# Sliding-window attention and sentence-level experts on one core: the first sentence alone to its gate, values behind their q/k, deeper prefetch, merged bank pairs, another slot order

## The chip, the cores and the metric

One core of one Trainium2 chip. The metric is the device time of an execution in microseconds (us); the span of a profile, from the first to the last instruction, is about 1.6 us shorter than the time of the same run. Engines: PE is the tensor engine (PEld its weight loads), DVE the vector engine, ACT the scalar engine, POOL GpSimd, SP the engine that here only issues transfers. With one core, a run is called slow when it takes over 1.5% longer than the fastest of the same kernel, so the label says how long it took, not why. Chips differ by a few tenths of a per cent (here, medians of the kernel before from 250.87 to 252.35 us); every kernel is therefore compared with runs of the kernel before on its own chip.

## The reference

```python
B, H, S, D = 8, 8, 576, 64          # q, k, v: float32
# 1. attention: causal, window of 64
scores = q @ k.T / 8 ;  keep 0 <= i - j < 64 ;  x = softmax(scores) @ v
# 2. one expert per sentence
x = x.transpose(0, 2, 1, 3).reshape(8, 576, 512)
logits = x.mean(axis=1) @ w_gate    # [8 sentences, 8 experts]
e = argmax(logits) ;  gate = softmax(logits)[e]
out = gate * (relu(x @ w1[e]) @ w2[e])          # w1: 512 x 1024, w2: 1024 x 512
```

In this draw the sentences choose the experts 5, 4, 2, 7, 1, 5, 7, 2. w1 is loaded eight times. w2 is kept on the core and loaded only at an expert's first use, so five times.

## The kernel before

A sentence is five units of attention: four pairs of heads (query rows 0 to 511), and one unit for the last 64 rows of all heads. For each pair: load q/k (POOL queue, cast to fp16 on the way) and values (SP queue), transpose q and k on PE, copy them out of PSUM, scores (`st_s`), exponential (ACT), mask (DVE), product with the values (`st_a`), division by the sum (DVE), transpose of the result (`st_x`). After five units the gate can be computed and the weights of the expert fetched. Expert work comes in chunks (`h_chunk`, 16 a sentence; `o_chunk`, 5 a sentence) that the program weaves between the pieces of attention, slot by slot.

```python
    qkp = tile_pool(name="qkp", bufs=6);  vp = tile_pool(name="vp", bufs=4)
    op_ = tile_pool(name="op", bufs=4)                     # output tiles
    ps_s = tile_pool(name="ps_s", bufs=1, space=PSUM)      # scores: 2 banks
    ps = tile_pool(name="ps", bufs=6, space=PSUM)          # everything else: 1 bank each
...
    def tr(n, part):                                       # half of a pair's q/k transposes
        tp = ps.tile([128, m, 2, 64], FP16, tag="b", name="tp")
        ...                                                # PE transposes into tp
        nc.vector.tensor_copy(out=qo, in_=tp[:, :, 0, :].rearrange("d t p -> d p t"))
        nc.scalar.copy(out=ko, in_=tp[:, :, 1, :].rearrange("d t p -> d p t"))
...
    def st_a(u, half):                                     # called twice a unit
        av = ps.tile([128, 512], FP32, tag="b", name="av")
        ...                                                # products; then reciprocal and multiply
...
    def o_chunk(i):                                        # i = 0..4
        ...                                                # 8 matmuls into po
        ob = op_.tile([128, Dm], FP32, tag="ob", name="ob")
        nc.vector.tensor_scalar(out=ob[0:n], in0=po[0:n], scalar1=gws[b][0:n, 0:1], ...)
        nc.sync.dma_start(out=out[b, 128 * i:128 * i + n, :], in_=ob[0:n])
...
        for s in range(NSLOT + 4):                         # START = 11: experts lag 11 slots
            st_a(s - 1, 0); st_a(s - 1, 1)
            fill(0.1)                                      # fill(p): expert chunks up to share p
            mask_it = st_s(s)
            fill(0.3)
            tr(n, 0);  mask_it()
            fill(0.5)
            st_x(s - 2)
            fill(0.75)
            tr(n, 1);  cast_v(n);  load_qk(n + 5);  load_v(n + 3)
            fill(1.0)
            if s >= 7 and (s - 7) % NU == 0: gate((s - 7) // NU)
            if s >= 8 and (s - 8) % NU == 0: gate2((s - 8) // NU)
```

The softmax here doesn't subtract the row's maximum and nothing guards it: scores larger than these inputs give would overflow.

## Time and profile before

| | kernel before |
|---|---|
| time, median of the first 6 runs | 251.97 us (249.93 to 252.39) |
| profiled span | 251.0 us |
| PE / DVE / ACT busy | 222.1 / 166.5 / 124.3 us |
| first expert matmul | 51.7 us |
| one sentence in the middle | 26.10 us |

The first view is the page of the kernel before: busy time of each engine, then PE in 40 slices of the span (tenths busy), then the clock granted to PE in the same slices.

```profile
PE 222.1 (89%) x2800; PEld 139.3 (56%) x2800; DVE 166.5 (66%) x525; ACT 124.3 (50%) x289; POOL 104.9 (42%) x191
...
PE   0476897779999999999999999999999998994992
...
PEclk9999999999999999999999999999999999999999
```

PE has gaps in the first nine slices and in the last seven, and none between. The windows of busy time of the kernel before (columns: stretch and length, then each engine's busy us and its number of instructions, granted clock, DMA share, GB/s) show one sentence of the middle:

```profile
106.34:132.44 26.10, 26.10 (x352) 15.92 (x352) 20.13 (x63) 15.00 (x37) 13.15 (x23) 1.00 1.11 219
```

PE is busy for all of it. The chain of waits of the kernel before (start, length, what) shows what bounds the ends:

```profile
7.65 12.99 DMA v_125<-in_v_dram
...
42.32 8.82 DMA w1t<-in_moe_w_dram
...
51.69 1.12 PE ph L327 x4
...
219.17 10.29 DMA w1t<-in_moe_w_dram
...
229.82 8.00 PE ph L327 x64
237.82 8.77 PE po L310 x40
```

The head waits for values, later for the first w1, and experts (`ph` is the first product, `po` the second) start at 51.7. The tail waits for the last w1.

The timeline of the kernel before (start, length, engine, line, operation, count, and in brackets the idle time before it with what ended it), one half of a pair's transposes:

```profile
108.30 0.41 PE L156 MATMUL tp<-ident,qk 128*64 128x128 f16 x8
...
108.75 0.44 DVE L161 COPY qT_151<-tp 128x256 f16<-128x256 f16 x1 [0.71 <-PE tp L156]
...
109.29 0.45 ACT L162 COPY kT_149<-tp 128x256 f16<-128x256 f16 x1 [0.30 <-DVE qT_151 L161]
```

ACT's copy of k starts 0.10 us after DVE's copy of q has ended, although it needs nothing from it. Both read the same PSUM tile.

### The profile page before, as it was taken

What the parts mean: (1) busy time and instruction counts of PE and PEld (TensorE: products, weight loads), DVE (VectorE), ACT (ScalarE), POOL (GpSimd) and SP (SyncE); (2) the same over time, 40 slices, a digit from 0 to 9 for tenths busy, and PEclk for the clock granted to TensorE, in tenths of its full rate; (3) what the DMA queues carried; (4) which work ended last, traced back from release to release, by engine and by line L of the source; (5) the groups of instructions that cost most, each with busy time, mean ns of one, the idle gap of its engine ahead of it and who ended that gap; (6) DMA issues with size and microseconds to landing.
All of it is one profiled execution on the core that took longest, in us unless ns stands there. A gap on an engine that the chain in (4) does not pass through costs nothing.

```text
span 251.0 us, 7513 instructions
## 1 busy us (share of the span) xinstructions
PE 222.1 (89%) x2800; PEld 139.3 (56%) x2800; DVE 166.5 (66%) x525; ACT 124.3 (50%) x289; POOL 104.9 (42%) x191
## 2 busy tenths in 40 slices
PE   0476897779999999999999999999999998994992
PEld 0364575546656665566556655665567546643741
DVE  3476898817687778776878787878686763441232
ACT  2265675636545764476537743764377425401500
POOL 7976996962195049514762468024500100000000
PEclk9999999999999999999999999999999999999999
DMA  6999999999399999999999999994930293087023
GB/s 123 209 206 185 200 178 190 185 204 207 67 153 217 199 306 147 222 200 298 164 216 199 293 170 206 199 296 81 216 115 4 31 207 123 1 146 209 3 86 102
DMA packets 59907, 42.45 MB, mean 169 GB/s; under 512 B 40416, under 2 KB 48608, under 8 KB 59872
## 3 DMA queue, kind: packets, MB, share of 16 engines
q0 software_dynamic: 16080, 23.07, 54.9%
q1 hardware_dynamic: 43792, 18.90, 30.0%
q8 instruction: 23, 0.38, 0.6%
q14 instruction: 12, 0.10, 0.1%
HBM read 61.88 MB, written 9.44 MB: 284 GB/s over the span
## 4 chain that ended last, share of the span: by engine, by line
PE 68%; DMA 16%; DVE 8%; SPq 3%; issue 2%; ACT 1%; POOLq 0%; DVEq 0%; ACTq 0%
PE ph L327 28%; PE po L310 21%; DMA w1t<-in_moe_w_dram 8%; PE tp L156 7%; DMA v_125<-in_v_dram 5%; PE sp L176 4%; PE av L211 3%; DMA out_dram<-ob 3%; PE xps L237 3%; SPq L77 2%; DVE x L195 2%; DVE pt L186 1%; PE av L220 1%; DVE ob L346 1%; PE gl L252 1%
## 5 line engine op out<-in xcount | busy, mean ns | idle before, releaser
L327 PE MATMUL ph<-xT,w1t 128*128 128x288 f16 x512 | 77.4, 292 | 6.4 <-DMA w1t<-in_moe_w_dram 5.4
L310 PE MATMUL po<-WT,hT 128*128 (+1 forms) x320 | 75.0, 380 | 0.0
L327 PEld LDWEIGHTS <-w1t 128*128 128x128 f16 x512 | 45.1, 99 | 20.8 <-DMA w1t<-in_moe_w_dram 6.1
L183 ACT ACTIVATE pt<-sp 128x1024 f16<-128x1024 f32 (+1 forms) x40 | 37.4, 935 | 24.1 <-PE sp L176 23.9
L332 ACT ACTIVATE hT<-ph 128x288 f16<-128x288 f32 x96 | 37.6, 413 | 22.6 <-PE ph L327 21.0
L310 PEld LDWEIGHTS <-hT 128*128 128x128 f16 (+1 forms) x320 | 29.9, 100 | 31.4 <-issue 0.8
L346 DVE TENSOR_SCALAR ob<-po,gw 128x512 f32<-128x512 f32 (+1 forms) x40 | 29.9, 748 | 23.6 <-PE po L310 20.9
L156 PE MATMUL tp<-ident,qk 128*64 128x128 f16 x576 | 33.1, 256 | 10.2 <-DMA qk<-in_k_dram 10.2
L195 DVE TENSOR_TENSOR x<-av,rl 128x256 f16<-128x256 f32 (+1 forms) x80 | 33.8, 423 | 2.7
L156 PEld LDWEIGHTS <-qk 128*64 128x64 f16 x576 | 22.1, 128 | 20.4 <-issue 17.8
L282 POOL DMA_DIRECT2D w1t<-in_moe_w_dram x8 | 6.0, 754 | 64.6 <-DVE x L195 42.1
L186 DVE TENSOR_TENSOR pt<-pt,mask 128x1024 f16<-128x1024 f16 (+1 forms) x40 | 27.0, 675 | 0.7 <-ACT pt L183 0.6
L239 ACT ACTIVATE xT<-xps 128x512 f16<-128x512 f16 x32 | 19.2, 601 | 14.7 <-PE xps L237 14.7
L334 DVE TENSOR_SCALAR hT<-ph 128x288 f16<-128x288 f32 x32 | 14.5, 452 | 17.2 <-PE ph L327 17.1
L66 POOL DMA_DIRECT2D qk<-in_q_dram x32 | 19.6, 613 | 13.8 <-PE av L211 8.1
L66 POOL DMA_DIRECT2D qk<-in_k_dram x32 | 19.5, 609 | 0.0
L211 PEld LDWEIGHTS <-pt 128*64 128x64 f16 x512 | 12.5, 122 | 9.9 <-DVE pt L186 8.1
L237 PE MATMUL xps<-ident,x 128*128 128x128 f16 (+1 forms) x160 | 16.7, 234 | 0.0
L237 PEld LDWEIGHTS <-x 128*128 128x128 f16 (+1 forms) x160 | 11.1, 105 | 8.9 <-issue 5.5
L194 DVE RECIPROCAL rl<-av 128x4 f32<-128x4 f32 (+1 forms) x80 | 13.6, 170 | 1.1 <-PE av L220 1.0
L162 ACT COPY kT_146<-tp 128x256 f16<-128x256 f16 (+1 forms) x12 | 5.5, 459 | 9.6 <-DVE qT_148 L161 9.4
L162 ACT COPY kT_149<-tp 128x256 f16<-128x256 f16 (+1 forms) x12 | 5.4, 452 | 8.6 <-DVE qT_151 L161 8.4
(234 smaller groups left out, 233.6 us busy)
## 6 DMA issues: line engine op xcount, KB each, us to landing
w1t<-in_moe_w_dram POOLq DMA_DIRECT2D x8, 1024.0 KB, 9.4
WT<-in_moe_w_dram POOLq DMA_DIRECT2D x8, 1024.0 KB, 15.0
out_dram<-ob SPq DMA_DIRECT2D x32, 256.0 KB, 7.1
qk<-in_q_dram POOLq DMA_DIRECT2D x32, 144.0 KB, 7.0
qk<-in_k_dram POOLq DMA_DIRECT2D x32, 144.0 KB, 8.1
out_dram<-ob SPq DMA_DIRECT2D x8, 128.0 KB, 5.5
v_100<-in_v_dram SPq DMA_DIRECT2D x2, 128.0 KB, 3.1
v_111<-in_v_dram SPq DMA_DIRECT2D x2, 128.0 KB, 7.5
```

What stands on the lines that cost most here:

```text
L66: nc.gpsimd.dma_start(out=t[64 * i:64 * i + 64].rearrange("p h t d -> p h (t d)"), in_=src[b, 2 * hp:2 * hp + 2, :, :].rearrange("h (p t) ...
L156: nc.tensor.transpose(out=tp[64 * hh:64 * hh + 64, t].rearrange("p a b -> p (a b)"), in_=qks[n][:, hh, lo + t, :], identity=ident)
L183: nc.scalar.activation(out=pv, in_=sp[:, :, 0:64 * m], func=AF.Exp, scale=scale)
L186: nc.vector.tensor_tensor(out=pv, in0=pv, in1=mk.unsqueeze(1).broadcast_to([128, 2, 64 * m]), op=ALU.mult)
L195: nc.vector.tensor_tensor(out=x.rearrange("p (g d) -> p g d", d=D), in0=avv[:, :, 0:D], in1=rl[0:n].broadcast_to([n, 4, D]), op=ALU.mult)
L211: nc.tensor.matmul(out=av[64 * jj:64 * jj + 64, o:o + D + 1], lhsT=pt[:, hh, 2 * i + jj, :], rhs=vx[:, 1 - jj, i, hh, :], start=True, stop ...
L237: nc.tensor.transpose(out=tp[:, g], in_=x[0:n, g, :], identity=ident[0:n, 0:n])
L239: nc.scalar.activation(out=xTs[b][:, c, 0:512], in_=tp.rearrange("p g t -> p (g t)"), func=AF.Copy, accum_out=pps[b][:, c:c + 1])
L310: m = nc.tensor.matmul(**kw)
L327: nc.tensor.matmul(out=ph[:, 0:SC], lhsT=w1v[:, kb, ft // 2, ft % 2, :], rhs=xTs[b][:, kb, ts(sc, SC)], start=(kb == 0), stop=(kb == NHP - 1))
L332: nc.scalar.activation(out=dst, in_=ph[:, 0:SC], func=AF.Relu)
L346: nc.vector.tensor_scalar(out=ob[0:n], in0=po[0:n], scalar1=gws[b][0:n, 0:1], scalar2=None, op0=ALU.mult)
```

## The change

Its intent: bring the first gate forward, so that PE gets expert work earlier; keep inputs ahead; and use fewer, larger instructions. The parts: (a) the five units of sentence 0 run alone, then its gate, and q/k go ahead of values in the first loads; (b) experts start at slot 8 for sentence 0 and lag 10 slots after that, gates follow the last unit at once, with the index going straight to w1's load; (c) deeper prefetch; (d) the merge: scores and products share two pairs of banks, one reciprocal and one multiply a unit, and each half of a pair's transposes is copied out, q and k together, by one engine; (e) another order inside a slot.

```diff
-    qkp = ... bufs=6    vp = ... bufs=4
+    qkp = ... bufs=10   vp = ... bufs=6
-    ps_s = ... bufs=1   ps = ... bufs=6
+    ps2 = ... bufs=2    ps = ... bufs=4
@@ load_v
+            if n < NHP:
+                tc.add_manual_dep(d.ins, qkd[n], SYNC, reason="order of the first loads")
@@ tr
-        nc.vector.tensor_copy(out=qo, in_=tp[:, :, 0, :].rearrange("d t p -> d p t"))
-        nc.scalar.copy(out=ko, in_=tp[:, :, 1, :].rearrange("d t p -> d p t"))
+        if part == 0:
+            nc.vector.tensor_copy(out=o, in_=i)          # q and k of this half
+        else:
+            nc.scalar.copy(out=o, in_=i)
@@ st_a: one call a unit
-        av = ps.tile([128, 512], FP32, tag="b", name="av")
+        av = ps2.tile([128, 2, 512], FP32, tag="s", name="av")
@@ the program (cut)
+        for u in range(1, NU + 2):                       # sentence 0 alone
+            tr(u, 0); mask_it(); tr(u, 1); mask_it = st_s(u); st_a(u - 1); cast_v(u)
+            ensure(min(u + 3, 7), min(u + 2, 6))         # q/k and values loaded so far ahead
+            st_x(u - 2)
+        gate(0)
+        for n in (NHP, NHP + 1): ensure(n + 4, n + 2); tr(n, 0); tr(n, 1); cast_v(n)
+        gate2(0); gate3(0)
+        for s in range(NU, NSLOT + 3):
+            rate = 2.4 if s < 15 else 3.3 if s < NSLOT - 6 else 2.4 if s < NSLOT else 1.2
+            st_a(s - 1); mask_it = st_s(s)
+            fill(0.4 * rate)
+            tr(n, 0); mask_it(); tr(n, 1); cast_v(n); ensure(n + 6, n + 4)
+            fill(0.3 * rate)
+            st_x(s - 2)
+            fill(0.3 * rate)
+            (gate and gate2 if s - 2 was a sentence's last unit, gate3 a slot later)
```

(Conditions at the ends, and the parts of the gate that only move, are cut.)

More of the change, by code (lines that the diff above doesn't have):

```diff
@@ L42 @@
     const = ctx.enter_context(tc.tile_pool(name="const", bufs=1))
-    qkp = ctx.enter_context(tc.tile_pool(name="qkp", bufs=6))
-    vp = ctx.enter_context(tc.tile_pool(name="vp", bufs=4))
+    qkp = ctx.enter_context(tc.tile_pool(name="qkp", bufs=10))
+    vp = ctx.enter_context(tc.tile_pool(name="vp", bufs=6))
     ptp = ctx.enter_context(tc.tile_pool(name="ptp", bufs=2))
@@ L51 @@
     gp = ctx.enter_context(tc.tile_pool(name="gp", bufs=2))
-    ps_s = ctx.enter_context(tc.tile_pool(name="ps_s", bufs=1, space=bass.MemoryType.PSUM))
-    ps = ctx.enter_context(tc.tile_pool(name="ps", bufs=6, space=bass.MemoryType.PSUM))
+    ps2 = ctx.enter_context(tc.tile_pool(name="ps2", bufs=2, space=bass.MemoryType.PSUM))
+    ps = ctx.enter_context(tc.tile_pool(name="ps", bufs=4, space=bass.MemoryType.PSUM))
     qks, v32s, v8s, xTs = {}, {}, {}, {}
     pts, xs, wts, gws, pps, eis, w1s = {}, {}, {}, {}, {}, {}, {}
+    qkd = {}
     NP = B * NHP
@@ L65, in load_qk @@
         for (i, src) in ((0, q), (1, k)):
-            nc.gpsimd.dma_start(
+            d = nc.gpsimd.dma_start(
                 out=t[64 * i:64 * i + 64].rearrange("p h t d -> p h (t d)"),
                 in_=src[b, 2 * hp:2 * hp + 2, :, :].rearrange("h (p t) d -> p h (t d)", t=TK))
+            qkd[n] = d.ins.name
     def load_v(n):
@@ L76, in load_v @@
         for hh in range(2):
-            nc.sync.dma_start(
+            d = nc.sync.dma_start(
                 out=t[:, :, hh, :],
                 in_=v[b, 2 * hp + hh, 0:512, :].rearrange("(i p) d -> p i d", p=128))
-        if hp == 0:
+            if n < NHP:
+                tc.add_manual_dep(d.ins, qkd[n], SYNC, reason="order of the first loads")
+        if hp == 3:
             t8 = vp.tile([128, H, D], FP32, tag="v8", name="v8", bufs=2)
@@ L92 @@
     load_qk(0)
-    load_v(0)
     nc.gpsimd.affine_select(out=ident, in_=ident, compare_op=ALU.not_equal, fill=1.0,
@@ L96 @@
     load_qk(1)
-    load_v(1)
+    load_qk(2)
     nc.gpsimd.affine_select(out=mask[0:64, 1:8], in_=mask[0:64, 1:8], compare_op=ALU.is_gt, fill=0.0,
@@ L101 @@
                             base=0, pattern=[[0, 8], [1, 64]], channel_multiplier=-1)
-    load_qk(2)
-    load_v(2)
     load_qk(3)
-    load_v(3)
-    load_qk(4)
+    for n in range(NHP):
+        load_v(n)
     wg = const.tile([128, NHP, E], FP32)
-    nc.sync.dma_start(out=wg, in_=moe_w_gate.rearrange("(kb p) e -> p kb e", p=128))
     iota = const.tile([1, E], FP32)
@@ L117 @@
     NT = 6
-    kTs, qTs = [], []
+    qkTs = []
     for m in range(NT):
-        t = const.tile([128, 64 + S], FP16, name=f"kT{m}")
-        nc.vector.memset(t[:, 0:64], 0.0)
-        kTs.append(t)
-        qTs.append(const.tile([128, S], FP16, name=f"qT{m}"))
+        t = const.tile([128, 2, 64 + S], FP16, name=f"qkT{m}")
+        nc.vector.memset(t[:, 1, 0:64], 0.0)
+        qkTs.append(t)
     NV = 4
@@ L158, in tr @@
                     in_=qks[n][:, hh, lo + t, :], identity=ident)
-        qo = qTs[n % NT].rearrange("d (p t) -> d p t", t=TK)[:, :, lo:hi]
-        ko = kTs[n % NT][:, 64:].rearrange("d (p t) -> d p t", t=TK)[:, :, lo:hi]
-        nc.vector.tensor_copy(out=qo, in_=tp[:, :, 0, :].rearrange("d t p -> d p t"))
-        nc.scalar.copy(out=ko, in_=tp[:, :, 1, :].rearrange("d t p -> d p t"))
+        o = qkTs[n % NT][:, :, 64:].rearrange("d a (p t) -> d a p t", t=TK)[:, :, :, lo:hi]
+        i = tp.rearrange("d t a p -> d a p t")
+        if part == 0:
+            nc.vector.tensor_copy(out=o, in_=i)
+        else:
+            nc.scalar.copy(out=o, in_=i)
     def st_s(u):
         b, c = divmod(u, NU)
-        sp = ps_s.tile([128, 2, 512], FP32, tag="s", name="sp")
+        sp = ps2.tile([128, 2, 512], FP32, tag="s", name="sp")
         pt = ptp.tile([128, 2, 8, 64], FP16, tag="pt", name="pt")
@@ L176, in st_s @@
                 nc.tensor.matmul(
-                    out=sp[:, hh, 64 * o:64 * o + 64], lhsT=kTs[n % NT][r, 64 * j:64 * j + 128],
-                    rhs=qTs[n % NT][r, 64 * j:64 * j + 64],
+                    out=sp[:, hh, 64 * o:64 * o + 64], lhsT=qkTs[n % NT][r, 1, 64 * j:64 * j + 128],
+                    rhs=qkTs[n % NT][r, 0, 64 + 64 * j:128 + 64 * j],
                     start=True, stop=True, tile_position=(64 * hh, 0), skip_group_check=True)
@@ L189, in st_s @@
         return apply_mask
-    def norm(u, av, n, x):
-        avv = av[0:n, 0:4 * (D + 1)].rearrange("p (g e) -> p g e", e=D + 1)
-        rl = gp.tile([128, 4, 1], FP32, tag="rl", name="rl")
-        nc.vector.reciprocal(out=rl[0:n], in_=avv[:, :, D:D + 1])
-        nc.vector.tensor_tensor(out=x.rearrange("p (g d) -> p g d", d=D), in0=avv[:, :, 0:D],
-                                in1=rl[0:n].broadcast_to([n, 4, D]), op=ALU.mult)
-    def st_a(u, half):
-        b, c = divmod(u, NU)
-        pt = pts[u]
-        if half == 0:
-            xs[u] = xp.tile([128, 4, 128], FP16, tag="x", name="x")
-        x = xs[u].rearrange("p i e -> p (i e)")[:, 256 * half:256 * half + 256]
-        av = ps.tile([128, 512], FP32, tag="b", name="av")
-        if c < NHP:
-            vx = vxs[(NHP * b + c) % NV]
-            for i in (2 * half, 2 * half + 1):
-                for hh in range(2):
-                    o = ((i % 2) * 2 + hh) * (D + 1)
-                    for jj in range(2):
-                        nc.tensor.matmul(
-                            out=av[64 * jj:64 * jj + 64, o:o + D + 1],
-                            lhsT=pt[:, hh, 2 * i + jj, :], rhs=vx[:, 1 - jj, i, hh, :],
-                            start=True, stop=True, tile_position=(0, 64 * jj),
-                            skip_group_check=True)
-            norm(u, av, 128, x)
-        else:
-            for g in range(4):
-                hp, hh = 2 * half + g // 2, g % 2
-                nc.tensor.matmul(
-                    out=av[0:64, g * (D + 1):(g + 1) * (D + 1)], lhsT=pt[:, hh, hp, :],
-                    rhs=vxts[b % 2][:, 2 * hp + hh, :], start=True, stop=True,
-                    skip_group_check=True)
-            norm(u, av, 64, x[0:64])
-        if half == 1:
-            pts.pop(u)
@@ new lines, in st_a @@
+    def st_a(u):
+        b, c = divmod(u, NU)
+        pt = pts.pop(u)
+        x = xp.tile([128, 4, 128], FP16, tag="x", name="x")
+        xs[u] = x
+        av = ps2.tile([128, 2, 512], FP32, tag="s", name="av")
+        n = 128 if c < NHP else 64
+        for g in range(8):
+            o = av[:, g // 4, (g % 4) * (D + 1):(g % 4 + 1) * (D + 1)]
+            i, hh = g // 2, g % 2
+            if c < NHP:
+                for jj in range(2):
+                    nc.tensor.matmul(
+                        out=o[64 * jj:64 * jj + 64], lhsT=pt[:, hh, 2 * i + jj, :],
+                        rhs=vxs[(NHP * b + c) % NV][:, 1 - jj, i, hh, :], start=True, stop=True,
+                        tile_position=(0, 64 * jj), skip_group_check=True)
+            else:
+                nc.tensor.matmul(out=o[0:64], lhsT=pt[:, hh, i, :], rhs=vxts[b % 2][:, g, :],
+                                 start=True, stop=True, skip_group_check=True)
+        avv = av[0:n, :, 0:4 * (D + 1)].rearrange("p a (g e) -> p a g e", e=D + 1)
+        rl = gp.tile([128, 2, 4, 1], FP32, tag="rl", name="rl")
+        nc.vector.reciprocal(out=rl[0:n], in_=avv[:, :, :, D:D + 1])
+        nc.vector.tensor_tensor(
+            out=x[0:n].rearrange("p i (h d) -> p (i h) d", d=D).rearrange(
+                "p (a g) d -> p a g d", a=2),
+            in0=avv[:, :, :, 0:D], in1=rl[0:n].broadcast_to([n, 2, 4, D]), op=ALU.mult)
@@ L256, in gate @@
         gm = gp.tile([1, 8], FP32, tag="gm", name="gm")
-        gi = gp.tile([1, 8], U32, tag="gi", name="gi")
+        gi = gp.tile([1, 8], U32, tag="gi", name="gi", bufs=4)
         nc.vector.max(out=gm, in_=gs)
         nc.vector.max_index(out=gi, in_max=gm, in_values=gs)
-        gf = gp.tile([1, 1], FP32, tag="gf", name="gf")
-        nc.vector.tensor_copy(out=gf, in_=gi[:, 0:1])
-        oh = gp.tile([1, E], FP32, tag="oh", name="oh")
-        nc.vector.tensor_scalar(out=oh, in0=iota, scalar1=gf, scalar2=None, op0=ALU.is_equal)
-        st2 = gp.tile([1, E], FP32, tag="st2", name="st2")
-        nc.vector.tensor_tensor(out=st2, in0=oh, in1=seen, op=ALU.mult)
-        nc.vector.tensor_tensor(out=seen, in0=seen, in1=oh, op=ALU.max)
-        ei = gp.tile([1, 2], U32, tag="ei", name="ei", bufs=4)
-        nc.vector.reduce_sum(out=gf, in_=st2, axis=AX.X)
-        nc.vector.tensor_copy(out=ei[:, 0:1], in_=gi[:, 0:1])
-        nc.vector.tensor_copy(out=ei[:, 1:2], in_=gf)
-        eis[b] = ei
         ereg = nc.gpsimd.alloc_register(f"er{b}")
-        nc.gpsimd.load(ereg, ei[0:1, 0:1])
-        hreg = nc.gpsimd.alloc_register(f"hr{b}")
-        nc.gpsimd.load(hreg, ei[0:1, 1:2])
+        nc.gpsimd.load(ereg, gi[0:1, 0:1])
         e = nc.gpsimd.snap(ereg, donate=True, min_val=0, max_val=E - 1)
-        have = nc.gpsimd.snap(hreg, donate=True, min_val=0, max_val=1)
         w1e = moe_w1.rearrange("e (kb p) f -> e p kb f", p=128)
-        w2e = moe_w2.rearrange("e (g p r) d -> e p g (r d)", p=128, r=2)
         w1t = wp.tile([128, NHP, F], FP16, tag="w1t", name="w1t")
@@ L282, in gate, with gate2 @@
         nc.gpsimd.dma_start(out=w1t, in_=w1e[ds(e, 1)].squeeze(0))
-        W2 = WT[:, ds(e, 1), :].squeeze(1).rearrange("p (g x) -> p g x", g=4)
-        mine = [nc.gpsimd.dma_start(out=W2, in_=w2e[ds(e, 1)].squeeze(0), cond=have < 1)]
-        for d in mine:
-            for other in tmms + loads:
-                tc.declare_no_dep(d.ins, other, reason="an expert is loaded before its first use")
-        loads.extend(d.ins.name for d in mine)
-        wts[b] = [d.ins.name for d in mine]
+        eis[b] = (gi, gs, gm, e)
+    def gate2(b):
+        gi, gs, gm, e = eis[b]
         nm = gp.tile([1, 1], FP32, tag="nm", name="nm")
@@ L297, in gate, with gate3 @@
         gws[b] = gr
-    def gate2(b):
+        gf = gp.tile([1, 1], FP32, tag="gf", name="gf")
+        nc.vector.tensor_copy(out=gf, in_=gi[:, 0:1])
+        oh = gp.tile([1, E], FP32, tag="oh", name="oh")
+        nc.vector.tensor_scalar(out=oh, in0=iota, scalar1=gf, scalar2=None, op0=ALU.is_equal)
+        st2 = gp.tile([1, E], FP32, tag="st2", name="st2")
+        nc.vector.tensor_tensor(out=st2, in0=oh, in1=seen, op=ALU.mult)
+        nc.vector.tensor_tensor(out=seen, in0=seen, in1=oh, op=ALU.max)
+        ei = gp.tile([1, 1], U32, tag="ei", name="ei")
+        nc.vector.reduce_sum(out=gf, in_=st2, axis=AX.X)
+        nc.vector.tensor_copy(out=ei, in_=gf)
+        hreg = nc.gpsimd.alloc_register(f"hr{b}")
+        nc.gpsimd.load(hreg, ei[0:1, 0:1])
+        have = nc.gpsimd.snap(hreg, donate=True, min_val=0, max_val=1)
+        w2e = moe_w2.rearrange("e (g p r) d -> e p g (r d)", p=128, r=2)
+        W2 = WT[:, ds(e, 1), :].squeeze(1).rearrange("p (g x) -> p g x", g=4)
+        mine = [nc.gpsimd.dma_start(out=W2, in_=w2e[ds(e, 1)].squeeze(0), cond=have < 1)]
+        for d in mine:
+            for other in tmms + loads:
+                tc.declare_no_dep(d.ins, other, reason="an expert is loaded before its first use")
+        loads.extend(d.ins.name for d in mine)
+        wts[b] = [d.ins.name for d in mine]
+    def gate3(b):
         glp = ps.tile([128, 1], FP32, tag="b", name="glp")
@@ L320, in h_chunk @@
                 pe = nc.tensor.alloc_register(f"pe{b}")
-                nc.tensor.load(pe, eis[b][0:1, 0:1])
+                nc.tensor.load(pe, eis[b][0][0:1, 0:1])
                 st["e"] = nc.tensor.snap(pe, donate=True, min_val=0, max_val=E - 1)
@@ L356, with ensure, start, fill @@
     NSLOT = B * NU
-    START = 11
-    RATE = 16.5 / NU
     chunks = []
+    spent = target = 0.0
+    qk_next, v_next = 4, 4
+    def ensure(nq, nv):
+        nonlocal qk_next, v_next
+        while qk_next <= min(nq, NP - 1):
+            load_qk(qk_next)
+            qk_next += 1
+        while v_next <= min(nv, NP - 1):
+            load_v(v_next)
+            v_next += 1
+    def start(b):
+        return 8 if b == 0 else NU * b + 10
+    def fill(amount):
+        nonlocal spent, target
+        target += amount
+        while chunks and spent < target:
+            cost, f = chunks.pop(0)
+            f()
+            spent += cost
+        if not chunks:
+            target = spent
     with tc.manual_schedule():
@@ L363 @@
         cast_v(0)
-        load_qk(5)
-        tr(1, 0)
-        tr(1, 1)
-        cast_v(1)
-        load_qk(6)
-        load_v(4)
-        spent = 0.0
-        for s in range(NSLOT + 4):
-            b, c = divmod(s, NU)
-            if s >= START and (s - START) % NU == 0 and (s - START) // NU < B:
-                chunks += list(moe_chunks((s - START) // NU))
-            def fill(part):
-                nonlocal spent
-                while chunks and spent < (s - START + part) * RATE:
-                    cost, f = chunks.pop(0)
-                    f()
-                    spent += cost
-            if 0 <= s - 1 < NSLOT:
-                st_a(s - 1, 0)
-                st_a(s - 1, 1)
-            fill(0.1)
+        nc.sync.dma_start(out=wg, in_=moe_w_gate.rearrange("(kb p) e -> p kb e", p=128))
+        mask_it = st_s(0)
+        for u in range(1, NU + 2):
+            if u < NHP:
+                tr(u, 0)
+                mask_it()
+                tr(u, 1)
+            elif u <= NU:
+                mask_it()
+            if u < NU:
+                mask_it = st_s(u)
+            if u <= NU:
+                st_a(u - 1)
+            if u < NHP:
+                cast_v(u)
+            ensure(min(u + 3, 7), min(u + 2, 6))
+            if u >= 2:
+                st_x(u - 2)
+        gate(0)
+        for n in (NHP, NHP + 1):
+            ensure(n + 4, n + 2)
+            tr(n, 0)
+            tr(n, 1)
+            cast_v(n)
+        gate2(0)
+        gate3(0)
+        for s in range(NU, NSLOT + 3):
+            b, c = divmod(s, NU)
+            for g in range(B):
+                if s == start(g):
+                    chunks += list(moe_chunks(g))
+            rate = 2.4 if s < 15 else 3.3 if s < NSLOT - 6 else 2.4 if s < NSLOT else 1.2
+            n = NHP * b + c + 2 if c < NHP else NP
+            if NU <= s - 1 < NSLOT:
+                st_a(s - 1)
             mask_it = st_s(s) if s < NSLOT else None
-            fill(0.3)
-            n = NHP * b + c + 2 if c < NHP else NP
+            fill(0.4 * rate)
             tr(n, 0)
@@ L392 @@
                 mask_it()
-            fill(0.5)
-            if 0 <= s - 2 < NSLOT:
-                st_x(s - 2)
-            fill(0.75)
             tr(n, 1)
@@ L399 @@
             if n < NP:
-                load_qk(n + 5)
-                load_v(n + 3)
-            fill(1.0)
-            if s >= 7 and (s - 7) % NU == 0:
-                gate((s - 7) // NU)
-            if s >= 8 and (s - 8) % NU == 0:
-                gate2((s - 8) // NU)
+                ensure(n + 6, n + 4)
+            fill(0.3 * rate)
+            if NU <= s - 2 < NSLOT:
+                st_x(s - 2)
+            fill(0.3 * rate)
+            if s > NU + 2 and (s - 2) % NU == 4:
+                gate((s - 2) // NU)
+                gate2((s - 2) // NU)
+            if s > NU + 3 and (s - 3) % NU == 4:
+                gate3((s - 3) // NU)
         for bb in range(B):
-            if START + NU * bb >= NSLOT + 4:
+            if start(bb) >= NSLOT + 3:
                 chunks += list(moe_chunks(bb))
```

## The prediction

> **What bounds the kernel now.** By the windows of busy time, from 52 to 207 us PE has no idle time: 26.10 us a sentence, again and again, with DVE at 20.1-20.5, ACT at 15.0 and a DMA share near 1.1. So the middle is bound by PE. PE is busy 222.1 of 251.0 us (page, part 1); nearly all of the 29 us of idle lies in 0-60 us (about 20) and after 200 us (about 9). In the head, the chain of waits runs over the values of the fourth head pair (landed at 20.6 us, DMA full from 2 us on), then over DVE at about 2.9 us a unit, then the first gate (arithmetic at 39.3-41.3 us), then the load of the first expert's w1 (issued 42.3, landed 51.1). Experts start at 51.7. In the tail PE waits 3.3 us for the last w1 (issued 219.2, after a gate whose sums were ready at about 212 but which queued behind 40 expert matmuls), about 1 us for the one before; then 4.4 us from the last product to the last output.
>
> **What the change does.**
> 1. Gate 0 comes after five units, not three later. At 2.9 us a unit, and with the index no longer passing through six small DVE operations (about 1 us), some 10 us earlier. q/k go ahead of values, so the fourth values should land near 17, not 20.6 (3.65 MB moved by then; sentence 0 needs 2.36 MB at about 190 GB/s). The Trainium skill (DMA: Bandwidth & Descriptors, Specifications) gives 512 B as the minimum transfer for line rate; here 40,416 of 59,907 packets are under that, and the head moves 180-210 GB/s against about 300 in slices with expert weights. The trace agrees: the head stays tied to bytes.
> 2. Merged operations: per unit one copy instead of two on each of DVE and ACT, one reciprocal (0.17) and one multiply (0.42) fewer, larger ones instead. Estimate from traced sizes: DVE -0.5 us a unit, ACT -0.2. This counts in the head only.
> 3. Estimate: gate 0 at 25-26, w1 landed at 36-37, experts start at about 37 with three units fewer behind them. PE work of a unit is (26.1-16.8)/5 = 1.9 us, so the head gains 15 - 6 = about 9 us.
> 4. Tail: gate 7 right after its last unit, two sentences of pure expert work left (16.8 us each, as the last one ran), both w1 loaded in time: about 4 us.
> 5. Costs: four PSUM tiles instead of six for transposes and expert products; a gate now waits on PE for its own copy and sum (about 1.4 us behind 1 us of filler), 0.5 us each; more DMA demand before 70 us (about 12.5 MB needed by then, what moved before). Together 2-4 us back.
>
> 252 - 9 - 4 - 1 (head DVE) + 3 = 241, less 2 for shorter slots in the head (an estimate): **239 us**. Range 231 to 246. Chances: faster by over 2% 0.93, within 2% 0.06, slower 0.01.
>
> **What would show it.** First expert matmul at 35-40 instead of 51.7; first w1 issue at 25-28; steady sentence still 26-26.5 with PE full; no PE wait for w1 at the end; last two experts back to back in about 34 us; DVE busy about 20 us less.
>
> **What would make it wrong.** If DMA cannot deliver in the head (deeper prefetch competes with the first w1 and w2), experts start at 42 or later, and it ends at 243-246. If four banks let PE wait for evacuations, the steady sentence rises above 27: +1 us a sentence costs 6. If slots 8-14 run at PE's pace and DVE relief counts, 231-234.

## The result, and the profile after

| | before | after |
|---|---|---|
| time, median | 250.97 us (20 runs, 248.52 to 253.21) | 247.57 us (10 runs, 244.13 to 250.40) |
| ratio of fast runs | | 0.981 [0.976, 0.986] |
| first expert matmul | 51.7 us | 43.1 us |
| one sentence in the middle | 26.10 us | 25.45 us |

A ratio is the mean time of one kernel's fast runs over that of the other's of the same rounds, so it is not quite the ratio of the medians; brackets are 95% intervals. The predicted range ended at 246. The interval lies on both sides of 0.98, so whether the gain reaches 2% is unclear. The spread is the first oddity: 6 us in 10 runs, where the kernel before had 4.7 us in 20 and the prediction nothing that varies.

The profiled run of the changed kernel (247.9 us of span) is one of its slow runs. Its page:

```profile
PE 215.0 (87%) x2800; PEld 140.8 (57%) x2800; DVE 154.4 (62%) x405; ACT 123.2 (50%) x257; POOL 103.7 (42%) x191
...
PE   0475676999889999299999999999998998999992
...
PEclk9999999999999999869999999999999999999998
```

There is a new hole in the middle of PE's row, in the 17th slice, and the clock falls there and in the next. The windows of the changed kernel (columns as before) give the hole, what follows it, and one sentence of the middle:

```profile
98.00:104.00 6.00, 2.56 (x38) 1.70 (x37) 0.00 (x0) 2.32 (x5) 2.34 (x6) 0.93 1.16 222
104.00:110.00 6.00, 4.99 (x37) 3.30 (x37) 3.60 (x7) 1.86 (x4) 0.53 (x1) 0.50 1.19 249
...
131.85:157.30 25.45, 25.34 (x351) 16.34 (x352) 18.89 (x48) 15.01 (x33) 12.36 (x22) 1.00 1.12 221
```

From 98 to 104 us DVE does nothing and PE is busy for 2.6 of 6 us; in the next 6 us the granted clock is 0.50. The chain of waits of the changed kernel names the cause:

```profile
31.33 8.53 DMA qk<-in_k_dram
...
43.22 2.03 PE ph L319 x8
...
88.60 15.51 DMA out_dram<-ob
104.21 0.75 DVE ob L338
105.01 1.12 PE ph L319 x4
...
226.44 7.95 PE ph L319 x64
234.38 8.76 PE po L302 x40
```

A sentence has five output tiles and there are four buffers. The fifth (DVE, 104.21) waited until the store of the first had landed, 15.5 us after its issue; behind it DVE stood still and then PE, which needed PSUM tiles that DVE had not emptied. The list of waits of the changed kernel (engine and line, what it waited for, us in total, times, longest):

```profile
DVE ob L338 <- DMA out_dram<-ob: 6.3, 1, 6.3
...
PE ph L319 <- DVE ob L338: 4.5, 1, 4.5
```

The kernel before has the same wait, shorter and late. Its list of waits:

```profile
DVE ob L346 <- DMA out_dram<-ob: 2.4, 2, 1.6
...
PE ph L327 <- DVE ob L346: 1.0, 1, 1.0
```

In its timeline the two waits of DVE end at 207.8 and 227.1 us, and that of PE at 208.5. So the ring was short before the change, and the trace said so.

The timeline of SP's queue in the changed kernel shows what the store had ahead of it:

```profile
82.86 4.10 SPq L79 DMA_DIRECT2D v_1716<-in_v_dram  x2
87.02 1.28 SPq L87 DMA_DIRECT2D v_1719<-in_v_dram  x1
88.60 0.42 SPq L340 DMA_DIRECT2D out_dram<-ob  x1
89.14 7.06 SPq L79 DMA_DIRECT2D v_1881<-in_v_dram  x2
96.69 4.07 SPq L340 DMA_DIRECT2D out_dram<-ob  x1
```

Value loads of 256-byte rows were issued just ahead of the store on the same queue, while w1 and w2 of the next expert (issued at 85.9 and 87.7) loaded through POOL's. The tail has the predicted signs: no wait for w1, and the last two experts run from 209.7 to 243.1, 33.4 us.

The copies of the transposes now overlap. Timeline of the changed kernel, one pair:

```profile
75.49 0.69 PE L154 MATMUL tp<-ident,qk 128*64 128x128 f16 x18
75.95 0.73 DVE L160 COPY qkT_146<-tp 128x512 f16<-128x512 f16 x1 [1.35 <-PE tp L154]
76.28 0.76 ACT L162 COPY qkT_146<-tp 128x640 f16<-128x640 f16 x1 [0.27 <-PE tp L154]
```

Each engine has a PSUM tile of its own and waits only for PE.

### The profile page after: what moved, and what is told of

Its sections match the earlier page's. It is cut to its first block, busy times and chain, and to the rows that moved or that the text cites. A ratio compares the mean times of both kernels' runs of the same rounds, so it can differ in the third digit from the quotient of the medians.

```text
span 247.9 us, 7329 instructions
## 1 busy us (share of the span) xinstructions
PE 215.0 (87%) x2800; PEld 140.8 (57%) x2800; DVE 154.4 (62%) x405; ACT 123.2 (50%) x257; POOL 103.7 (42%) x191
## 4 chain that ended last, share of the span: by engine, by line
PE 69%; DMA 15%; DVE 8%; issue 3%; POOL 3%; ACT 1%; SPq 0%; POOLq 0%; DVEq 0%
PE ph L319 26%; PE po L302 24%; DMA out_dram<-ob 6%; PE tp L154 5%; DMA qk<-in_k_dram 5%; PE av L203 4%; PE sp L176 3%; PE xps L227 3%; DVE ob L338 2%; DMA v_114<-in_v_dram 2%; DMA v_569<-in_v_dram 2%; DVE pt L186 2%; PE av L208 1%; PE gl L242 1%; DVE x L213 1%
## 5 line engine op out<-in xcount | busy, mean ns | idle before, releaser
L319 PE MATMUL ph<-xT,w1t 128*128 128x288 f16 x512 | 73.7, 294 | 4.5 <-DVE ob L338 4.5
L319 PEld LDWEIGHTS <-w1t 128*128 128x128 f16 x512 | 47.7, 100 | 18.7 <-issue 5.2
L302 PEld LDWEIGHTS <-hT 128*128 128x128 f16 (+1 forms) x320 | 30.6, 100 | 31.2 <-issue 0.8
L256 POOL DMA_DIRECT2D w1t<-in_moe_w_dram x8 | 6.0, 753 | 75.9 <-DVE oh L272 69.3
L154 PE MATMUL tp<-ident,qk 128*64 128x128 f16 x576 | 26.8, 251 | 6.7 <-DMA qk<-in_k_dram 6.7
L154 PEld LDWEIGHTS <-qk 128*64 128x64 f16 x576 | 21.2, 129 | 13.0 <-issue 11.2
L213 DVE TENSOR_TENSOR x<-av,rl 128x512 f16<-128x512 f32 (+1 forms) x40 | 27.6, 690 | 1.4
L186 DVE TENSOR_TENSOR pt<-pt,mask 128x1024 f16<-128x1024 f16 (+1 forms) x40 | 26.0, 650 | 0.0
L212 DVE RECIPROCAL rl<-av 128x8 f32<-128x8 f32 (+1 forms) x40 | 8.0, 199 | 13.7 <-PE av L203 11.2
L162 ACT COPY qkT_142<-tp 128x640 f16<-128x640 f16 x6 | 4.5, 754 | 7.9 <-PE tp L154 7.6
L160 DVE COPY qkT_142<-tp 128x512 f16<-128x512 f16 x6 | 4.3, 722 | 5.8 <-PE tp L154 5.8
```

The source lines that it names most:

```text
L154: nc.tensor.transpose(out=tp[64 * hh:64 * hh + 64, t].rearrange("p a b -> p (a b)"), in_=qks[n][:, hh, lo + t, :], identity=ident)
L186: nc.vector.tensor_tensor(out=pv, in0=pv, in1=mk.unsqueeze(1).broadcast_to([128, 2, 64 * m]), op=ALU.mult)
L213: nc.vector.tensor_tensor(out=x[0:n].rearrange("p i (h d) -> p (i h) d", d=D).rearrange("p (a g) d -> p a g d", a=2), in0=avv[:, :, :, 0:D ...
L302: m = nc.tensor.matmul(**kw)
L319: nc.tensor.matmul(out=ph[:, 0:SC], lhsT=w1v[:, kb, ft // 2, ft % 2, :], rhs=xTs[b][:, kb, ts(sc, SC)], start=(kb == 0), stop=(kb == NHP - 1))
```

## The experiments

All outputs are right. First a table by position in time, read from the timelines of PE: first expert matmul, start of the second sentence's experts, a sentence in the middle, and the span; then the ratio to the kernel before. The span is that of the one profiled run, the ratio that of all fast runs. The subsections follow it.

| run | what it is | first expert | second | middle | span | ratio |
|---|---|---|---|---|---|---|
| before | | 51.7 | 80.2 | 26.1 | 251.0 | 1 |
| after, slow run | the change | 43.1 | 73.9 | 25.4 | 247.9 | 0.981 [0.976, 0.986] |
| a0_b, a0_c | the change | 44.2, 43.3 | 75.1, 74.5 | 25.4 | 243.4, 243.0 | one time each |
| a1_ob8 | + 8 output tiles | 43.3 | 74.3 | 25.4 | 241.2 | 0.969 [0.965, 0.973] |
| a7_ob5 | + 5 output tiles | 43.5 | 74.5 | 25.4 | 241.4 | 0.967 [0.963, 0.972] |
| b1_merged | before + merge | 47.9 | 75.6 | 26.1 | 248.5 | 0.994 [0.990, 0.999] |
| b2_layout | before + slot order | 52.2 | 79.2 | 25.5 | 246.7 | 0.987 [0.978, 0.995] |
| b4_merge_layout | before + both | 48.9 | 75.9 | 25.5 | 245.3 | 0.975 [0.972, 0.979] |
| a5_ob8_unmerged | a1 without merge | 46.4 | 77.9 | 26.0 | 247.7 | 1.001 [0.993, 1.008] |
| a6_pairs_only | a1 with copies unmerged | 46.7 | 80.0 | 26.6 | 252.7 | 1.010 [1.007, 1.013] |
| e1_ahead | best version | 40.7 | 71.0 | 25.4 | 237.9 | 0.957 [0.952, 0.962] |

### The wait for an output tile: a0_again, a0_b, a0_c, a1_ob8, a7_ob5

a0_again, a0_b and a0_c are the changed kernel, unaltered. The edit of the other two:

```diff
-    op_ = tile_pool(name="op", bufs=4)
+    op_ = tile_pool(name="op", bufs=8)      # a1_ob8;  5 in a7_ob5
```

> The changed kernel unaltered, to see its spread on one chip beside its variants and to get a second trace. Theory A (the fifth output tile of an expert waits for an output buffer whose store is stuck behind input traffic): a wait of some us for an output store stands in the trace somewhere before 110 us, with a dip of the granted clock just after it; time 244-250 and spread over several us. Rival B (the slow runs are only a lower clock of the chip, no wait): the clock is low over the whole span and no wait for a store over 1 us.

> Changed kernel with eight output buffers instead of four. Theory A: the wait for a store goes, with it the dip of the clock; 5-7 us faster than the changed kernel in its slow runs, median 240-243. Rival B (clock of the chip): no change, 244-250. Rival C (DMA is short of bandwidth before 110 us whatever waits first): the wait moves to q/k, values or w1 and the gain is under 2 us.

> Changed kernel with five output buffers, one for each output tile of a sentence. If the wait is only for the sentence's own first store: gone, 0.969 as with eight, spread about 1 us. If stores of the sentence before still hold buffers: some of the wait stays, 0.97-0.98 and a wider spread.

> The changed kernel again, to catch a trace of one of its fast runs (both traces so far are of slow ones, with waits of 6 us for an output store). If the wait is what separates its slow runs from its fast ones: in a fast run (243-246 us) the wait for a store is under 3 us, and the granted clock has no dip before 110 us or a shorter one. If fast runs show the same wait, the spread has another cause.

> The same once more, for the same reason: a slow run (over 247.5) shows a wait for a store of 4-7 us and a dip of the clock behind it, a fast one under 3 us.

Measured. a0_again: 245.46 us, 243.29 to 250.84, ratio 0.976 [0.971, 0.981]; its profiled run was again slow and had a wait of 6.6 us for a store. The two later looks (245.00 and 244.64 us, single runs, so their state is unknown) show the same wait, shorter. The list of waits of a0_b:

```profile
DVE ob L338 <- DMA out_dram<-ob: 2.6, 1, 2.6
...
PE ph L319 <- DVE ob L338: 1.2, 1, 1.2
```

In a0_c it is 4.5 us in two waits, and PE waits 1.3 us. PE's idle time is then about 1.3 us instead of 4.5 to 4.8, and the clock has no dip in either run; the sentence that starts at 100 us takes 26.8 and 26.9 us, its neighbours 25.4 to 25.5, where in the slow profile it took 32.4 (99.4 to 131.8). With eight tiles the wait is gone from the trace: 243.06 us, 242.78 to 243.76. With five it is gone too: 242.88, 242.22 to 245.45, a spread of 3.2 us where about 1 was expected. Expected of a1_ob8 was a median of 240 to 243, so the gain is just short of that.

What follows: theory A stands. The ring of output tiles, one short for a sentence, costs the changed kernel 0.7% even between fast runs on one chip (0.976 to 0.969, with intervals that overlap a little), and some 5 us more (247.9 against 243.2 us of span) in the two traced slow runs, in which the wait was long and PE's clock fell behind it. One tile more removes it. Rival B, a lower clock of the chip as such, falls: the clock falls after the hole, not over the run, and not at that place in the traces without a long hole (a0_b, a0_c, a1_ob8, a7_ob5). The slow runs that were not traced are taken to be of the same kind; that is not shown.

### Why the store takes so long: a4_actstore

```diff
-            nc.sync.dma_start(out=out[b, 128 * i:128 * i + n, :], in_=ob[0:n])
+            nc.scalar.dma_start(out=out[b, 128 * i:128 * i + n, :], in_=ob[0:n])
```

> Changed kernel, four output buffers, but the stores are issued from ScalarE's queue instead of behind the value loads on SyncE's. If the store that holds the ring waits behind value loads in the same queue: it lands in under 10 us instead of 15.5, the wait before 110 us goes, 241-243. If all DMA is slow together at that time (bandwidth): still about 15 us to land, the wait stays, 244-250. If issuing costs ScalarE too much: exponentials late, over 246 without a wait for a store.

Measured: 252.52 us, ratio 1.002 [0.997, 1.007]. The landing times of the stores, first of the changed kernel:

```profile
DMA to landing us min/median/max: 2.0/5.6/15.8
```

and of a4_actstore:

```profile
DMA to landing us min/median/max: 2.0/5.8/8.6
```

No output tile waited for a store any more. So the store was late because value loads were queued ahead of it, and not because all DMA was slow: the bytes are the same in both runs, and DMA moved 219 GB/s in the sentence of the late store (73.9 to 99.4) and 216 in the same sentence here (80.2 to 105.7). The Trainium skill (DMA: Bandwidth & Descriptors, "Issuing engines are not separate DMA queues") says that issuing from several engines saves only the sequencer's time; here it nearly halved the longest landing. The same page ("Queues, rings and completion order") has SP and ACT each own rings, from which transfers are taken in order. The trace of the changed kernel agrees as to the order: the values issued just ahead of the store landed at 97.6 and 102.7, the store at 104.1, the values issued behind it at 107.6 and 108.1. But the move is a bad bargain: ACT must wait for DVE's output tile before it can issue the store, and everything behind stands still. The list of waits of a4_actstore:

```profile
ACT xT L229 <- DVE ob L338: 11.5, 6, 2.5
```

A middle sentence took 25.4 to 26.2 us and the first one 35.7 (44.5 to 80.2). The third alternative of the expectation came true together with the first one's landing and wait; the first one's time, 241 to 243, did not.

### The prefetch: a2_shallow

```diff
-    qkp = ... bufs=10   vp = ... bufs=6     ensure(n + 6, n + 4)
+    qkp = ... bufs=6    vp = ... bufs=4     ensure(n + 5, n + 3)
```

> Changed kernel with the prefetch depth of before (6 q/k and 4 value buffers, 5 and 3 pairs ahead). If the deeper prefetch is what holds up the output stores (theory A with the prefetch as its cause): the wait for the store goes and the time is 241-244. If the stores are held up by the weights and the values needed anyway: unchanged, 244-250. If the depth is needed in the short slots: PE waits for q/k or values and it is slower, over 250.

Measured: 251.42 us, ratio 1.003 [0.997, 1.008]. The wait for the store is gone, but the depth is needed: sentence 0's experts took from 43.3 to 82.3. The chain of waits of a2_shallow:

```profile
36.27 17.65 DMA v<-in_v_dram
```

Values were loaded so late that they met the first w1 and w2. The first outcome (wait gone) and the third (slower) came together; the deeper prefetch is worth more than the wait it brings.

### What the merge and the slot order are worth: b1_merged, b2_layout, b4_merge_layout, a5_ob8_unmerged, a6_pairs_only

```diff
b1_merged        before, with (d) alone: bank pairs, merged copies and products
b2_layout        before, with (e) alone:
-            fill(0.1); st_s(s); fill(0.3); tr(n, 0); mask; fill(0.5); st_x; fill(0.75); tr(n, 1) ...; fill(1.0)
+            st_s(s); fill(0.4); tr(n, 0); mask; tr(n, 1) ...; fill(0.7); st_x; fill(1.0)
b4_merge_layout  before, with (d) and (e)
a5_ob8_unmerged  after, eight output tiles, without (d)
a6_pairs_only    after, eight output tiles; of (d) only the copies undone:
-        if part == 0: nc.vector.tensor_copy(out=o, in_=i)
-        else: nc.scalar.copy(out=o, in_=i)
+        nc.vector.tensor_copy(out=o[:, 0], in_=i[:, 0])
+        nc.scalar.copy(out=o[:, 1], in_=i[:, 1])
```

> The kernel before with only the merged bank pairs, merged copies and merged products. My prediction: no effect in the middle, 1 us in the head, 0.99-1.00 of the time before. Rival (the steady sentence fell from 26.10 to 25.45 us because of the merge): 4-6 us faster, about 246.

> The kernel before, only with the changed kernel's order inside a slot: both transpose parts together, expert work in three places instead of five. The steady sentence is 26.10 us in before and in the merged-only run, 25.4-25.5 in the changed kernel. If the slot order is the cause: 25.4-25.6 a sentence and 3-4 us off the time, 0.985. If not (then the lag of the experts or the prefetch): 26.1 and 0.995-1.00.

> The kernel before with the merge and the changed slot order, but the old head, lag, prefetch and gate. Merge alone gave 0.994, slot order alone 0.987. If the first-sentence-alone head is what makes the changed kernel fast: 0.98 or more here. If these two parts carry it (in the traces the merged-only kernel starts its second expert at 75.6, the changed one with eight buffers at 74.3 but with one unit fewer behind it): 0.970-0.978, steady sentence 25.4-25.5.

> Changed kernel with eight output buffers but without the merged bank pairs, copies and products. In the merged-only run of before the merge brought experts 3.8 us earlier in the trace and 0.6% of the time. If it pays only in the head: gate 0 and experts 1-4 us later than 27.8 and 43.3, steady sentence 25.4-25.5, 0.975-0.985. If it also carries the middle: steady over 25.8.

> Changed kernel with eight output buffers, bank pairs and merged products kept, but the transposes' copies split again over VectorE (q) and ScalarE (k), two each. Merged all: 0.969; nothing merged: 1.001. If the products' pair carries it: 0.97-0.98. If the copies do: 0.99-1.00.

Measured, as in the table. Four things follow.

First, in the kernel before the shorter sentence comes from the slot order, alone or with the merge. The windows of b2_layout:

```profile
130.10:155.60 25.50, 25.29 (x357) 16.29 (x351) 19.89 (x63) 15.02 (x37) 12.55 (x21) 1.00 1.13 221
```

and of b1_merged, one sentence each:

```profile
127.80:153.90 26.10, 26.10 (x356) 15.92 (x351) 18.95 (x49) 14.90 (x34) 13.10 (x23) 1.00 1.10 218
```

The matmuls are the same; PE's busy time falls by 0.8 us when they come in fewer, longer stretches. That each change between kinds of matmul costs PE something fits, but no run measured it by itself.

Second, the new head is worth little. The kernel before with merge and slot order, old head, old lag and old prefetch, reached 0.975. The whole change with eight output tiles has 0.969, and as written, with four, 0.981 and 0.976. So of what the change could give, about 0.6% is left for (a), (b) and (c) together (two chips, and intervals that overlap; a7_ob5, on the chip of b4_merge_layout, gives 0.967 against 0.975, and intervals that touch), and the missing output tile eats it.

Third, in the changed program the merge is worth over 3%, against 0.6% in the old one: 1.001 without it, 0.969 with it. By the table 3.1 us are in the head (46.4 to 43.3) and about 0.5 us a sentence in the middle. In the head of a5_ob8_unmerged PE waited 9.2 us for ACT's copies of k, against 5.4 for all copies in the head of the changed kernel. In its middle (129.8 to 155.8) PE was busy for 25.30 of 26.00 us and had one wait, 0.7 us for the gate's sum on DVE. So the half microsecond of the middle is a late gate sum and not a PSUM tile, and the slot order alone doesn't give 25.4 in this program.

Fourth, most of it is the copies: with bank pairs and merged products but the copies split again, the kernel is slower than with nothing merged (which shares six PSUM tiles, the products among them, where this one shares four), and experts start as late as there (46.7 and 46.4). The timeline of a6_pairs_only, one pair:

```profile
134.80 0.69 PE L154 MATMUL tp<-ident,qk 128*64 128x128 f16 x18
135.26 0.45 DVE L159 COPY qkT<-tp 128x256 f16<-128x256 f16 x1 [1.35 <-PE tp L154]
...
135.80 0.45 ACT L160 COPY qkT<-tp 128x256 f16<-128x256 f16 x1 [0.48 <-DVE qkT L159]
...
136.20 0.49 DVE L159 COPY qkT<-tp 128x320 f16<-128x320 f16 x1
...
136.77 0.46 ACT L160 COPY qkT<-tp 128x320 f16<-128x320 f16 x1 [0.53 <-DVE qkT L159]
```

and its list of waits for PE in that sentence:

```profile
PE ph L317 <- ACT qkT L160: 1.0, 2, 0.5
```

A PSUM tile that two engines empty is handed from one to the other, and is free only at 136.25 and 137.23; in the changed kernel both were free by 77.04, 0.9 us after PE had finished, against 1.7 here. Four tiles are then too few and PE waits for one: 1.0 of the 1.1 us that this sentence is longer. The Trainium skill (PSUM — Partial Sum Buffer, "PSUM bank collisions raise a hardware error") says that two engines may not read one bank of the same partitions at once, and that the compiler orders such accesses; the traces agree in that ACT's copy of a shared tile never began before DVE's had ended (64 copies each in before, b2_layout, a5_ob8_unmerged and a6_pairs_only; the shortest gap is 0.03 us). Whether the wait is kept for that reason, no run shows.

### The head: c1_nodep, c2_qk9, c3_warm, c4_warm2, d1_best, e1_ahead

All have eight output tiles.

```diff
c1_nodep   values do not wait for q/k:
-            if n < NHP: tc.add_manual_dep(d.ins, qkd[n], SYNC, reason="order of the first loads")
c2_qk9     q/k of the pairs 8 and 9 ahead of the first w1:
-            ensure(min(u + 3, 7), min(u + 2, 6))
+            ensure(min(u + 3, 9), min(u + 2, 6))
c3_warm    matmuls on a constant tile, results unused: 11 at the start, 3 after each pair's
           transposes and 3 before each st_a, more around the gate
c4_warm2   the same, but 5 after each pair's transposes and none before st_a
d1_best    c2_qk9, and gate3(0) two slots later
e1_ahead   d1_best, and in the head
-            tr(u, 0); mask_it(); tr(u, 1); mask_it = st_s(u); st_a(u - 1); cast_v(u)
+            mask_it(); mask_it = st_s(u); tr(u + 1, 0); tr(u + 1, 1); cast_v(u - 1); st_a(u - 1)
           (and the loads of q/k and values are issued one unit later)
```

> Eight output buffers, and the first values no longer wait for the q/k of their pair to land. Base: the changed kernel with eight buffers (0.969 of before, experts from 43.3 us). If that wait costs the head (VectorE sat 3.6 us until the first values at 10.9 us): first values land near 8.5, experts start 2-3 us earlier, 0.96. If the order pays as intended (q/k first is worth more): experts start later, 0.975-0.98.

> Eight output buffers, and the q/k of pairs 8 and 9 are loaded before the first w1 and not behind it. If the ninth pair's q/k (landed at 40.0) holds up the experts: they start near 40 instead of 43.3, 0.957-0.96. If w1 itself is what arrives last and only moves later by the bytes put ahead of it: start 42-44, 0.966-0.972.

> Eight output buffers, and 60 or so matmuls on a constant tile (results unused) in the head to keep TensorE busy, so that its clock is granted full before 43 us. If the head is a chain through a half-speed TensorE (18 transposes take 1.17 us there, 0.69 later): transposes at 0.69 in the head, first gate near 24 instead of 27.8, experts near 39-40, 0.955-0.96. If the head is bound by arrivals of q/k and values: gate at 27-28 as before, 0.968 or worse.

> Eight output buffers, constant-tile matmuls put only where TensorE waits anyway (5 after each pair's transposes, none between scores and products): a cleaner form of the run in which the added matmuls took as long as the faster clock saved. If the head is a chain through a half-speed TensorE: transposes 0.69, units 2.8-3.0 us apart instead of 3.6, gate 0 at 24-25. If the chain is elsewhere: gate 0 at 27-28. Experts gain less than the gate, as w1 still takes 9 us.

> Eight output buffers, q/k of pairs 8 and 9 before the first w1, and the broadcast of the first gate's weight (TensorE waited about 2 us for it) two slots later. Expected: experts start at 40-41 instead of 43.3, w1's landing last; 0.955-0.962 of before, 239-241 us. If w1 lands at 42 or later: 0.964, no better than the run with the q/k alone.

> On the version with eight output buffers, early q/k and the late broadcast (0.964): in the head each pair's transposes go one unit further ahead and the value casts stand after the mask, so that a unit's scores wait for nothing of the unit before. If the head's 3.6 us a unit is a serial chain through the program order: 2.7-3.0 us a unit, gate 0 at 24-26, experts at 38-40, 0.952-0.96. If it is arrivals: gate at 27-28, 0.964.

| run | first gate's matmuls | first expert | time | ratio |
|---|---|---|---|---|
| a1_ob8 | 27.8 | 43.3 | 243.06 | 0.969 [0.965, 0.973] |
| c1_nodep | 28.2 | 44.5 | 243.39 | 0.965 [0.960, 0.970] |
| c2_qk9 | 27.6 | 42.1 | 242.41 | 0.964 [0.959, 0.969] |
| c3_warm | 27.4 | 44.1 | 245.02 | 0.976 [0.970, 0.982] |
| c4_warm2 | 29.2 | 45.3 | 245.09 | 0.978 [0.970, 0.985] |
| d1_best | 28.1 | 41.8 | 241.61 | 0.964 [0.956, 0.972] |
| e1_ahead | 27.4 | 40.7 | 240.14 | 0.957 [0.952, 0.962] |

The gate does not come earlier, whatever is done: 27.4 to 29.2. That rules out the order of values and q/k (c1), which costs or gives nothing that these runs resolve: in c1_nodep the first values were cast at 8.1 us instead of 10.9, as expected, and the gate still came at 28.2. Nor do arrivals hold the rest of the head: in the changed kernel the fourth pair's values had landed at 15.2 us, 12.5 us before the gate. Of the expectations for the start, c2_qk9 met its second outcome (42.1, in 42 to 44; its ratio lies between the two), c1_nodep met neither (1.2 us later, ratio no worse), and d1_best missed (41.8 for 40 to 41, 0.964 for 0.955 to 0.962, though w1 had landed at 40.1).

The two runs with added matmuls are a failed experiment. PE did run at full clock for much of the head in c3_warm (18 transposes in 0.69 us at 17.1, where the changed kernel takes 1.17), but the added matmuls stand in PE's order, took about 1.6 us a unit, and so cost what the clock saved. In c4_warm2 the clock fell back in places (16 products in 0.65 us at 16.7, in 0.45 at 20.3). Whether half speed holds up the head stays open.

e1_ahead missed its expectation for the gate and met the others: experts at 40.7 (expected 38 to 40), 0.957 (0.952 to 0.96). Its units were about 3.1 us apart in place of 3.6, yet the gate came at 27.4. The timeline of PE in e1_ahead shows the last part:

```profile
20.46 0.40 PE L176 MATMUL sp<-qkT 64*128 64x64 f16 x8
21.88 0.94 PE L203 MATMUL av<-vx,pt 128*64 128x65 f16 x16 [1.02 <-DVE pt L186]
...
24.20 0.65 PE L208 MATMUL av<-vxt,pt 128*64 128x65 f16 x8 [0.84 <-DVE pt L186]
...
25.87 0.39 PE L227 MATMUL xps<-ident,x 64*128 64x64 f16 x4 [0.47 <-DVE x L213]
27.37 0.35 PE L242 MATMUL gl<-wg,pl 128*1 128x8 f32 x8 [1.11 <-DVE pl L235]
```

From the last scores to the gate it is 6.9 us of one step after another, with nothing left to overlap: exponential, mask, product, division, transpose, copy, sum. After the gate, w1 is issued 2.2 us later and takes 8.8 us; three more units run at the head's pace meanwhile, and they end last, at 40.7. My reason for predicting 25 to 26, a rate of engines, does not describe a head that ends in a chain.

e1_ahead is the fastest version found: 240.14 us, against 251.25 of the kernel before on the same chip. Its interval lies apart from that of a1_ob8, but not from those of c2_qk9 and d1_best, so which of the three edits of the head earns it is not settled. One of its six runs (243.55) was slow.

## Why the prediction was right or wrong

The prediction was 239 with a range of 231 to 246; measured were 247.57.

1. *"What bounds the kernel now."* Right for the middle and for the last w1. In the tail, "about 1 us for the one before" is no wait for w1: it is PE's wait of 1.0 us at 208.5 behind a store, so the wait that the change then lengthened was in the trace and was misread. For the head, 2.9 us a unit was read as DVE's pace, which a lighter DVE would quicken; it was not seen that a head is a chain, and that PE runs at half speed there (18 transposes in 1.17 us in the head, 0.69 later), though what that costs stays open. "The head stays tied to bytes" failed: the fourth values landed at 15.2, earlier than the predicted 17, and the gate came late all the same.
2. *Costs (point 5).* This is the step that put the time outside the range: the list of costs has PSUM tiles, gates and DMA demand, and no word of the output tiles. Four buffers for five tiles a sentence had cost the kernel before 1.0 us of PE. Measured: 0.7% between fast runs on one chip, and holes of 4.5 us with a half-speed clock behind them in slow ones. How many runs are slow decides the median: a0_again, the same kernel with one slow run of six, had 245.46, inside the range. The demand for DMA before 70 us was named, but as a delay of the experts' start; what it hit was a store of an expert already running, at 88 to 105 us.
3. *The head (point 3): experts at 37, "gains 15 - 6 = about 9 us".* The term that was mis-sized is the start: 43.1 to 45.2 in the four traces of the changed kernel, so 6.5 to 8.6 gained and not 15, of which 6 are owed for three units not yet done: 0.5 to 2.6 us are left of the 9. The merge alone, with the old head and nothing owed, brings 3.8 (experts at 47.9). Gate 0 came at 27.8 (predicted 25 to 26), as units were about 3.6 us apart and not 2.9; its w1 was issued at 30.0 (25 to 28) and landed at 38.0 (36 to 37). But w1 was not the last to be waited for: units 5 to 7, which the program puts ahead of the experts, took until 43. Even with the output tiles mended, 243.06 is 4 us above the prediction. That this lies in the range that the prediction gave for a DMA that can't deliver (243 to 246, experts at 42 or later) is luck: w1 took 8.1 us against 8.8 before, and PE waited only 0.7 us for q/k between w1's issue and the experts.
4. *Merged operations (point 2): "This counts in the head only."* Wrong in the changed program, where the merge is worth 3.2%. Counting DVE's saved time in the head missed two effects: a tile that one engine empties is done earlier than one that two empty in turn, and the gate's sum in the middle is not late. DVE's busy time fell by 12 us, not by 20.
5. *"Steady sentence still 26-26.5."* It fell to 25.45. The slot order stood in the diff and was not costed; alone it is worth 1.3%.
6. *Tail (point 4).* Right in its signs: no wait for w1, the last two experts in 33.4 us (predicted 34). Its size was not measured by itself. PE's waits in the tail fell from 4.3 us (3.3 and 1.0) to 1.8, now before the last two gates, so about 2.4 us of the 4 can be seen.

Where the expected gain went: part was never there (the head), part was lost to a longer wait (the output tile), and two gains of an unexpected size (slot order, merged copies) kept the kernel ahead: without the merge, and with the output tiles mended, it is no faster than before (1.001).

## What to carry to other kernels

When work is moved earlier or packed closer, go through every ring of buffers, those of the outputs too, and ask whether it holds one round of the work at the slowest landing in the trace; here one more tile of 256 KB was worth about as much as (a), (b) and (c) together. Look for the wait in the trace before: a short one can be there already. Where PSUM tiles are few or the copies stand in a chain, give each tile to one engine to empty, rather than a share to each of two. And price the start of a kernel by its chain of steps with durations taken from the start, not by engine rates from the middle.

## What the Trainium skill lacked or had wrong

- DMA: Bandwidth & Descriptors, "Issuing engines are not separate DMA queues": it says that a second issuing engine saves only the sequencer's time. For the landing of a single transfer that is too little: stores behind 256-byte-row value loads on one queue took up to 15.8 us to land, on ACT's queue at most 8.6.
- None of the pages consulted says what a store queued behind loads means for a ring of output buffers: 15.5 us from issue to landing, in a sentence of 25.4 us.
- TensorE: Matmul & The Clock Gate, "Part 1: The HAM clock gate": half speed by default and after idle time, full after about 3.4 us of activity. The trace agrees as to half speed: 0.50 granted after a hole of 4.5 us. It stayed so for at least 4.4 us of activity (105.0 to 109.4), longer than the page's figure. The section warns that the clock events of a trace can be unreliable. What it lacks is that a profile's clock row may then hide the half speed: here the row reads 9 throughout the head, in which PE ran at half speed, as these lines of PE's timeline of the changed kernel show (head, after the start of the experts, after the hole):

```profile
28.05 2.13 PE L154 MATMUL tp<-ident,qk 128*64 128x128 f16 x36
...
45.18 0.69 PE L154 MATMUL tp<-ident,qk 128*64 128x128 f16 x18
...
106.06 1.17 PE L154 MATMUL tp<-ident,qk 128*64 128x128 f16 x18
```

- PSUM — Partial Sum Buffer, "PSUM bank collisions raise a hardware error": right as far as seen, but it doesn't say what sharing costs in time: ACT idled a median of 0.53 us before its copies of a shared tile in a6_pairs_only, 0.27 before its copies in the changed kernel, and splitting the copies of both halves made the kernel 4% slower (0.969 to 1.010).
